# A fused attention and gated MLP block: even and odd positions in paired tiles, products by pairs, and a new order where one chunk hands over to the next

## The chip, the core and the metric

The kernel runs on one core of a Trainium2 chip. The core has a matrix engine (TensorE, in profiles "PE", with its weight loads as "PEld"), a vector engine (VectorE, "DVE"), an activation engine (ScalarE, "ACT"), a third elementwise engine (GpSimd, "POOL") and a queue engine that issues most of the DMA transfers (SyncE, "SP"). Each engine works through its own instructions in order and waits on semaphores for the others. The metric is the device time of one execution in microseconds (us). Lower is better.

## The reference

The input is one sequence of 2048 positions with 512 features, all in float32.

```python
xn = layernorm(x)
# A: 32 heads of 16, each query sees 8 keys: its own position and those 2, 4, ..., 14 earlier
q, k, v = split(xn @ wqkv)
logits = einsum(q, k at pos - 2*w) * 16**-0.5      # masked to -1e9 where pos - 2*w < 0
s = (softmax(logits) applied to v at pos - 2*w) @ wo
# B: an MLP with squared relu, 512 -> 1792 -> 512
h = relu(xn @ w1 + b1)**2
g = silu(h @ w2 + b2)
return x + s * g
```

## The kernel before, in words

Every float32 product is made from three products of a rounded "high" part and a remainder "low" part (`PASSES`): high by high, high by low, low by high. So a 128x512 output with 512 inner features takes 4 x 3 = 12 matmuls. The low part of a tensor is a subtraction on the vector engine or on GpSimd after a rounding copy on the activation engine.

**First phase.** The 2048 positions are 16 tiles of 128 (`NT`). For each tile t the rows of x are loaded (`load_x`, L127), normalised (`mean`, `spread` and `norm` on the activation engine with small steps on GpSimd), transposed on TensorE (`trans`) and split (the high part is the copy in `trans`, the low part `lowx` on the vector engine). Then three products of 12 matmuls give q, k and v (`qkv`, s = 0, 1, 2). Each result goes from PSUM to a staging tile `stg` (an activation copy) and from there to DRAM scratch `sq`, `sk`, `sv` (L395): 256 KB per store, in pieces of 512 bytes, since the scratch is laid out in 4 groups of 128 features. The transposed, split tile itself is stored to `sx` for the later chunks (L537). Four PSUM banks (`psA`) take the products, two (`psT`) the transposes.

**Attention** runs on the vector engine, in 8 units of 256 positions (`UP`). A unit loads its q, and k and v with a halo of 14 positions, with eight consecutive positions in each partition (L197), so a unit needs two finished tiles. It does 4 multiplications and 4 reductions for the logits, the softmax, and 4 multiplications and 4 reductions for the result, which is stored to `so` (L257). `attention()` is a generator: `pump(margin)` takes steps from it as long as a running price of the vector engine's work stays below that of TensorE plus a margin (`SLACK`, `LATE`, `ROOM`). So the order on each engine is fixed when the program is built; only the DMA issues are placed by a scheduler, by when it expects their data.

**Second phase.** The MLP runs in 4 chunks of 512 positions (`C`). For each of the 14 blocks f of 128 hidden features, `up(c, f)` makes 12 matmuls into `ph` (two PSUM banks, `psH`), the activation engine does relu and two squares, and `lowh(f)` on the vector engine makes the low part of `h` out of the same PSUM bank. `up(c, f + 2)` writes that bank again and so waits for `lowh(f)`. `down(pb, f, j)` adds block f to the four outputs `pb` (the four `psA` banks), two blocks behind `up`. `out_product` multiplies attention results by wo into `pw`. At the end of a chunk come `down` of the last two blocks, `gate` (add b2 on the vector engine, silu on the activation engine) and the first two `up` of the next chunk. The chunk's input `xU` (1 MB) is loaded from `sx` right behind the last `up` of the chunk before, into the one buffer `xT` (L401). `finish` multiplies s by g, adds x and stores the rows of the output (L604).

## Time and profile before

| What | us |
|---|---|
| three timed runs | 505.92, 505.95, 511.05 (median 505.95) |
| the profiled execution, its own time | 505.65 |
| its span, first to last instruction | 503.9 |
| TensorE busy | 495.0 (98%) |
| vector engine busy | 414.8 (82%) |
| activation engine busy | 214.2 (43%) |
| GpSimd busy | 113.7 (23%) |
| q, k, v stores | 48 of 256 KB |
| mean granted TensorE clock | 0.998 |

The profiled execution's own time is 1.75 us above its span and 0.3 us below the median of the runs. In timelines a row is a start, a duration and the work, with the idle time of the engine before it and what ended that idle time in brackets; the duration of a group of matmuls includes the modelled end of the last one, so from start to start is the better measure of pace. "SPq" and "ACTq" rows are DMA issues.

### The profile page before, as it was taken

The numbers are of one execution on the slowest core, as the hardware profiler recorded it, in microseconds if no ns is written. First come the engines' busy times: TensorE is split into PE (matmuls) and PEld (weight loads), VectorE is DVE, ScalarE is ACT, GpSimd is POOL, SyncE is SP. The second block draws the span as 40 slices with busy tenths as digits, with TensorE's granted clock in tenths as the row PEclk, the third lists the DMA queues.
The fourth block names the chain that finished last, engine by engine and source line by source line (L and its number), as shares of the span: only waits on it lengthen the run. The fifth ranks groups of instructions, "written<-read, shape, count | busy, mean of one in ns | idle before, by whom it ended". The sixth has DMA issues, their size and how long they took to land.

```text
span 503.9 us, 5987 instructions
## 1 busy us (share of the span) xinstructions
PE 495.0 (98%) x2209; PEld 408.5 (81%) x2209; DVE 414.8 (82%) x327; ACT 214.2 (43%) x393; POOL 113.7 (23%) x127
## 2 busy tenths in 40 slices
PE   7999999999999999999999999999999999999996
PEld 6788888888888888887888888788888888888886
DVE  5309999999999999988899998779999978952245
ACT  3965366663333655512622441263234136123321
POOL 3632165572000589400203000020300002110000
PEclk9999999999999999999999999999999999999999
DMA  8899787899947757461441417044242604021022
GB/s 302 242 285 338 239 280 244 303 312 317 343 140 230 206 160 212 121 261 63 126 157 64 177 42 283 41 148 134 86 174 56 249 1 145 23 85 40 2 85 84
DMA packets 62089, 85.65 MB, mean 170 GB/s; under 512 B 5372, under 2 KB 45676, under 8 KB 59244
## 3 DMA queue, kind: packets, MB, share of 16 engines
q1 hardware_dynamic: 61196, 78.98, 48.4%
q10 hardware_dynamic: 864, 6.29, 3.2%
q8 instruction: 17, 0.28, 0.2%
q14 instruction: 12, 0.10, 0.1%
HBM read 57.94 MB, written 27.32 MB: 169 GB/s over the span
## 4 chain that ended last, share of the span: by engine, by line
PE 91%; DMA 5%; ACT 1%; DVE 1%; issue 0%; ACTq 0%; POOL 0%; POOLq 0%
PE ph L74 30%; PE pb L74 28%; PE pq L74 25%; PE pw L74 7%; DMA xU<-sx 4%; PE pxT L74 2%; DVE xn L74 1%; DMA x<-in_A_x 1%; ACT wq L74 0%; ACT scratch L74 0%; ACT xT L74 0%; ACT stg L74 0%; DVE z L74 0%; ACT xn L74 0%; DVE st L74 0%
## 5 line engine op out<-in xcount | busy, mean ns | idle before, releaser
L74 PE MATMUL pb<-w,h 128*128 128x512 f32 x672 | 161.1, 389 | 0.0
L74 PEld LDWEIGHTS pb<-w,h 128*128 128x128 f32 x672 | 126.2, 188 | 26.2
L74 PE MATMUL ph<-xU,w 128*128 128x512 f32 x504 | 120.8, 389 | 1.5 <-DMA xU<-sx 1.5
L74 ACT ACTIVATE ph<-ph,b1t 128x512 f32<-128x512 f32 x56 | 37.0, 661 | 197.5 <-PE ph L74 184.7
L74 PEld LDWEIGHTS ph<-xU,w 128*128 128x128 f32 x504 | 94.4, 188 | 21.8 <-issue 2.3
L74 PE MATMUL pq<-wq,xt 128*128 128x512 f32 x432 | 101.3, 392 | 0.0
L74 PEld LDWEIGHTS pq<-wq,xt 128*128 128x128 f32 x432 | 80.4, 188 | 16.4
L74 DVE TENSOR_TENSOR pr<-k,q 128x2048 f32<-128x2048 f32 x32 | 75.9, 2370 | 12.2 <-DMA k<-sk 11.8
L74 DVE TENSOR_TENSOR h<-ph,h 128x512 fp32r<-128x512 f32 x56 | 38.4, 685 | 45.7 <-ACT ph L74 45.7
L74 DVE TENSOR_TENSOR pv<-v,L 128x2048 f32<-128x2048 f32 x32 | 73.9, 2310 | 0.6
L74 DVE TENSOR_REDUCE L<-pr 128x128 f32<-128x2048 f32 x32 | 73.1, 2283 | 0.7
L74 DVE TENSOR_REDUCE v<-pv 128x256 f32<-128x2048 f32 x32 | 72.9, 2280 | 0.6
L74 POOL TENSOR_TENSOR z<-z,xr 128x512 f32<-128x512 f32 x12 | 19.2, 1613 | 221.6 <-DVE z L74 214.9
L74 PE MATMUL pw<-wot,oT 128*128 128x512 f32 (+1 forms) x204 | 45.5, 376 | 0.0
L74 ACT ACTIVATE stg<-pq 128x512 f32<-128x512 f32 x48 | 28.3, 595 | 39.0 <-PE pq L74 35.7
L74 PEld LDWEIGHTS pw<-wot,oT 128*128 128x128 f32 x204 | 36.8, 188 | 7.1
L74 POOL TENSOR_TENSOR w<-w1r,w 128x512 fp32r<-128x512 f32 x14 | 28.0, 2003 | 55.4 <-DMA rwo<-in_A_wo 48.9
L74 PE MATMUL ph<-xT,w 128*128 128x512 f32 x168 | 40.5, 390 | 0.0
L74 PEld LDWEIGHTS ph<-xT,w 128*128 128x128 f32 x168 | 31.5, 188 | 6.7
L74 PE MATMUL pq<-wq,xT 128*128 128x512 f32 x144 | 36.4, 410 | 0.0
L74 ACT ACTIVATE h<-ph 128x512 fp32r<-128x512 f32 x56 | 33.5, 599 | 1.8
L74 ACT ACTIVATE ph<-ph 128x512 f32<-128x512 f32 x56 | 33.3, 595 | 0.0
(54 smaller groups left out, 318.7 us busy)
## 6 DMA issues: line engine op xcount, KB each, us to landing
k<-sk SPq DMA_DIRECT2D x8, 1408.0 KB, 8.4
v<-sv SPq DMA_DIRECT2D x8, 1408.0 KB, 7.0
sx<-xt SPq DMA_DIRECT2D x12, 512.0 KB, 4.6
xU<-sx ACTq DMA_DIRECT2D x6, 1024.0 KB, 6.9
x<-in_A_x SPq DMA_DIRECT2D x16, 256.0 KB, 4.1
sq<-stg SPq DMA_DIRECT2D x16, 256.0 KB, 4.4
q<-sq SPq DMA_DIRECT2D x8, 512.0 KB, 4.1
sk<-stg SPq DMA_DIRECT2D x16, 256.0 KB, 4.7
```

Source lines behind the costliest of these rows:

```text
L74: return tc.keep_in_program_order(f(*a, **k))
```

## The change

**Positions.** Tile 2i and tile 2i + 1 no longer hold 128 consecutive positions each. Together they hold 256 consecutive positions, the first tile the even ones and the second the odd ones, so partition p of the pair holds positions 2p and 2p + 1. The loads of x, the residual loads and the output stores use rows two apart. The staging tile now holds one of q, k, v for both tiles of a pair ([P, 4, 2, P], four buffers instead of two of [P, 3, 4, P]), and one DMA of 512 KB stores it, in pieces of 1 KB: 24 stores instead of 48. The loads of the attention result `oq` read 1 KB pieces as well, and the last residual load pieces of 4 KB.

**Order in the first phase.** The products go by pairs: q of both tiles, k of both, v of both, with the transposes, statistics and the splitting of the MLP weights placed anew between them.

**Hand-over of chunks.** `down` of both last blocks now stands ahead of the first two `up` of the next chunk, and `lowh(0)` stands behind the four gates instead of ahead of the second `up`.

```diff
+    def tile_rows(a, t):
+        return a[t // 2 * UP:(t // 2 + 1) * UP, :].rearrange("(p e) d -> e p d", e=2)[t % 2]
...
-    def qkv(t, s, stg, between=None):
+    stgs = {}
+
+    def qkv(t, s, between=None):
+        if t % 2 == 0:
+            stgs[s] = pstg.tile([P, 4, 2, P], F32, name=f"stg{t}_{s}", tag="stg", bufs=4)
         ps = psA(f"pq{t}_{s}")
...
-        A.activation(stg[:, s].rearrange("p g c -> p (g c)"), ps, AF.Copy, scale=0.25 if s == 0 else 1.0)
-        dst = (sq, sk, sv)[s]
-        r0 = t * P + (0 if s == 0 else HALO)
-        dma(dst[:, r0:r0 + P, :].rearrange("g p c -> p g c"), stg[:, s])
-        done_tiles["qk" if s < 2 else "v"] = t + (s > 0)
+        A.activation(stgs[s][:, :, t % 2], ps.rearrange("p (g c) -> p g c", g=4), AF.Copy,
+                     scale=0.25 if s == 0 else 1.0)
+        if t % 2:
+            r0 = (t - 1) * P + (0 if s == 0 else HALO)
+            dst = (sq, sk, sv)[s][:, r0:r0 + UP, :].rearrange("g (p e) c -> p g (e c)", e=2)
+            dma(dst, stgs[s].rearrange("p g e c -> p g (e c)"))
+            done_tiles["qk" if s < 2 else "v"] = t + (s > 0)
...
-    qkv_tile(0, 1, second)
+    qkv(0, 1, lambda: highs(2, 0))
+    trans(2)
+    norm(3)
     lowx(2)
...
-    for t in range(2, NT):
...
+    for a in range(2, NT, 2):
+        b, more = a + 1, a + 2 < NT
...
+        qkv(a, 0)
+        if more:
+            trans(a + 2)
         pump(LATE)
...
+        qkv(b, 0)
+        weights(a - 5)
+        if more:
+            lowx(a + 2)
+            trans(b + 2)
...
+        qkv(a, 1)
...
+        if more:
+            lowx(b + 2)
+        pump(LATE)
+        if not more:
             up(0, 0)
+        qkv(b, 1)
...
+        qkv(a, 2)
...
+        qkv(b, 2)
...
+        if a >= TPC:
+            for t in (a, b):
+                dma(sx[t // TPC][:, t % TPC], xt.pop(t).bitcast(F32))
...
                 for j in range(TPC):
                     down(pb, NF - 2 + i, j)
                 pump()
-                if i:
-                    lowh(0)
+            for i in range(2):
                 up(c + 1, i)
             for j in range(TPC):
                 gate(c, j, pb)
+            lowh(0)
             lowh(1)
             pump()
```

Two places show how instructions move. First TensorE at the hand-over from chunk 0 to chunk 1 (`pw` are the products with wo, `pb0` the outputs of chunk 0, `ph1_0` to `ph1_2` the first `up` products of chunk 1 and `xU1` its input; `h0_13` is the last hidden block of chunk 0). Before:

```order
L74 MATMUL pw1_2050<-wot_1509,oT1_1913 128x512 x12
L74 MATMUL pb0_0_1510<-w12_1744,h0_12_1976 128x512 x3
L74 MATMUL pb0_1_1511<-w12_1744,h0_12_1976 128x512 x3
L74 MATMUL pb0_2_1512<-w12_1744,h0_12_1976 128x512 x3
L74 MATMUL pb0_3_1513<-w12_1744,h0_12_1976 128x512 x3
L74 MATMUL ph1_0_2086<-xU1_2014,w0_637 128x512 x12
L74 MATMUL pb0_0_1510<-w13_1793,h0_13_2017 128x512 x3
L74 MATMUL pb0_1_1511<-w13_1793,h0_13_2017 128x512 x3
L74 MATMUL pb0_2_1512<-w13_1793,h0_13_2017 128x512 x3
L74 MATMUL pb0_3_1513<-w13_1793,h0_13_2017 128x512 x3
L74 MATMUL ph1_1_2121<-xU1_2014,w1_719 128x512 x12
L74 MATMUL ph1_2_2155<-xU1_2014,w2_803 128x512 x12
```

The same place on TensorE after the change:

```order
L74 MATMUL pw1_2034<-wot_1493,oT1_1897 128x512 x12
L74 MATMUL pb0_0_1494<-w12_1728,h0_12_1960 128x512 x3
L74 MATMUL pb0_1_1495<-w12_1728,h0_12_1960 128x512 x3
L74 MATMUL pb0_2_1496<-w12_1728,h0_12_1960 128x512 x3
L74 MATMUL pb0_3_1497<-w12_1728,h0_12_1960 128x512 x3
L74 MATMUL pb0_0_1494<-w13_1777,h0_13_2001 128x512 x3
L74 MATMUL pb0_1_1495<-w13_1777,h0_13_2001 128x512 x3
L74 MATMUL pb0_2_1496<-w13_1777,h0_13_2001 128x512 x3
L74 MATMUL pb0_3_1497<-w13_1777,h0_13_2001 128x512 x3
L74 MATMUL ph1_0_2084<-xU1_1998,w0_661 128x512 x12
L74 MATMUL ph1_1_2101<-xU1_1998,w1_756 128x512 x12
L74 MATMUL ph1_2_2136<-xU1_1998,w2_825 128x512 x12
```

The first product that reads `xU1` has moved behind one more group of 12 matmuls, and the three `ph1` products now follow each other without other work between them.

The vector engine at the same hand-over (`pv` and `v` are attention steps, `z` rows that read `pb` the gates, `h1_0` and `h1_1` the low parts of the next chunk's first two blocks). Before:

```order
L74 TENSOR_TENSOR pv3_1_2115<-v3_1835,L3_1412 128x4x2x256
L74 TENSOR_REDUCE v3_1835<-pv3_1_2115 128x256
L74 TENSOR_TENSOR pv3_2_2118<-v3_1835,L3_1412 128x4x2x256
L74 TENSOR_TENSOR h1_0_2099<-ph1_0_2086,h1_0_2099 128x512
L74 TENSOR_TENSOR z0_0_2138<-pb0_0_1510,b2t_141 128x512
L74 TENSOR_TENSOR z0_1_2141<-pb0_1_1511,b2t_141 128x512
L74 TENSOR_TENSOR z0_2_2144<-pb0_2_1512,b2t_141 128x512
L74 TENSOR_TENSOR z0_3_2147<-pb0_3_1513,b2t_141 128x512
L74 TENSOR_TENSOR h1_1_2134<-ph1_1_2121,h1_1_2134 128x512
L74 TENSOR_TENSOR z0_0_2138<-z0_0_2138,pw0_2037 128x512
```

After:

```order
L74 TENSOR_TENSOR pv3_1_2082<-v3_1819,L3_1396 128x4x2x256
L74 TENSOR_TENSOR z0_0_2118<-pb0_0_1494,b2t_141 128x512
L74 TENSOR_TENSOR z0_1_2121<-pb0_1_1495,b2t_141 128x512
L74 TENSOR_TENSOR z0_2_2124<-pb0_2_1496,b2t_141 128x512
L74 TENSOR_TENSOR z0_3_2127<-pb0_3_1497,b2t_141 128x512
L74 TENSOR_TENSOR h1_0_2097<-ph1_0_2084,h1_0_2097 128x512
L74 TENSOR_TENSOR h1_1_2114<-ph1_1_2101,h1_1_2114 128x512
L74 TENSOR_TENSOR z0_0_2118<-z0_0_2118,pw0_2021 128x512
```

The low part of `h1_0` stands behind the four gates now, and two attention steps have left the stretch ahead of them.

TensorE at the start of the program (`pq0_1` is k of tile 0, `pq1_1` k of tile 1, `pxT2` and `pxT3` the transposes of tiles 2 and 3, `wq1` and `wq2` the split weights of k and v). Before:

```order
L74 MATMUL pq1_0_233<-wq0_111,xT0_170 128x512 x12
L74 MATMUL pq0_1_267<-wq1_112,xT0_170 128x512 x6
L74 MATMUL pxT2_276<-ident_75,xn2_256 128x128 x4
L74 MATMUL pq0_1_267<-wq1_112,xT0_170 128x512 x6
L74 MATMUL pq1_1_301<-wq1_112,xT0_170 128x512 x12
L74 MATMUL pxT3_341<-ident_75,xn3_282 128x128 x4
L74 MATMUL pq0_2_351<-wq2_113,xT0_170 128x512 x12
```

After:

```order
L74 MATMUL pq1_0_231<-wq0_111,xT0_170 128x512 x12
L74 MATMUL pq0_1_266<-wq1_112,xT0_170 128x512 x12
L74 MATMUL pxT2_282<-ident_75,xn2_254 128x128 x4
L74 MATMUL pq1_1_299<-wq1_112,xT0_170 128x512 x12
L74 MATMUL pxT3_339<-ident_75,xn3_288 128x128 x4
L74 MATMUL pq0_2_350<-wq2_113,xT0_170 128x512 x12
```

The transposes of tile 2 have moved from the middle of k of tile 0 to its end.

More of the change, by code (lines that the diff above doesn't have):

```diff
@@ L424, in lowh @@
         V.tensor_sub(h[:, 1], ph, h[:, 0].bitcast(F32))
-    def qkv_tile(t, s, between=None):
-        if s == 0:
-            stgs[t] = pstg.tile([P, 3, 4, P], F32, name=f"stg{t}", tag="stg", bufs=2)
-        qkv(t, s, stgs[t], between)
-    stgs = {}
     sts = [px.tile([P, 6], F32, name=f"st{t}", tag="st", bufs=2) for t in range(2)]
@@ L472, in first @@
         mean(2)
-    def second():
-        highs(2, 0)
-        trans(2)
-        norm(3)
-    qkv_tile(0, 0, first)
+    qkv(0, 0, first)
     lowx(1)
@@ L482, in body @@
     spread(2)
-    qkv_tile(1, 0, lambda: highs(1, 2))
+    qkv(1, 0, lambda: highs(1, 2))
     lows(1, 2)
@@ L491, in body @@
     mean(4)
-    qkv_tile(1, 1, lambda: highs(2, 2))
+    qkv(1, 1, lambda: highs(2, 2))
     lows(2, 2)
@@ L497, in body @@
     next(stream)
-    qkv_tile(0, 2, lambda: norm(4))
+    qkv(0, 2, lambda: norm(4))
     mean(5)
@@ L502, in body, with weights @@
     pump(LATE)
-    qkv_tile(1, 2)
-    mean(6)
+    qkv(1, 2)
+    norm(5)
     pump(LATE)
-    for t in range(2, NT):
-        f = t - 5
-        if 0 <= f < NKEEP:
-            load_w(keep, f)
-        if t + 3 < NT:
-            norm(t + 3)
-        qkv_tile(t, 0)
-        if t + 2 < NT:
-            trans(t + 2)
-        if t + 4 < NT:
-            spread(t + 4)
-        pump(LATE)
-        if t == NT - 1:
+    for a in range(2, NT, 2):
+        b, more = a + 1, a + 2 < NT
+        later = a + 4 < NT
+        def weights(f):
+            if 0 <= f < NKEEP:
+                load_w(keep, f)
+            if 0 <= f - 1 < NKEEP:
+                split_w(f - 1)
+        if later:
+            mean(a + 4)
+        qkv(a, 0)
+        if more:
+            trans(a + 2)
+        pump(LATE)
+        qkv(b, 0)
[3 more added lines that the diff above has]
+            trans(b + 2)
+        if later:
+            mean(b + 4)
+        pump(LATE)
+        qkv(a, 1)
+        if later:
+            spread(a + 4)
+        if more:
+            lowx(b + 2)
+        pump(LATE)
+        if not more:
             up(0, 0)
-        qkv_tile(t, 1)
-        if t + 5 < NT:
-            mean(t + 5)
-        if t == NT - 1:
+        qkv(b, 1)
+        if later:
+            spread(b + 4)
+        if not more:
             pump()
@@ L526, in body @@
             lowh(0)
-        if 0 <= f - 1 < NKEEP:
-            split_w(f - 1)
-        if t + 2 < NT:
-            lowx(t + 2)
+        weights(b - 5)
         pump(LATE)
-        qkv_tile(t, 2)
-        if t == NT - 4:
+        qkv(a, 2)
+        if later:
+            norm(a + 4)
+        pump(LATE)
+        qkv(b, 2)
+        if later:
+            norm(b + 4)
+        if a == NT - 4:
             dma(b1t, b1.rearrange("(f p) -> p f", p=P))
             dma(b2t, b2[None, :].to_broadcast([P, D]))
-        if t >= TPC:
-            dma(sx[t // TPC][:, t % TPC], xt.pop(t).bitcast(F32))
-        pump(LATE if t < NT - 1 else -SLACK)
+        if a >= TPC:
+            for t in (a, b):
+                dma(sx[t // TPC][:, t % TPC], xt.pop(t).bitcast(F32))
+        pump(LATE if more else -SLACK)
     lowh(1)
@@ L595, in load_r @@
         xrs[t] = p2.tile([P, D], F32, name=f"xr{t}", tag="xr", bufs=2)
-        dma(xrs[t], x[t * P:(t + 1) * P, :])
+        dma(xrs[t], tile_rows(x, t))
     def finish(t, eng, xt=None, cols=slice(0, D)):
```

15 lines of the change are left out of this document (8 added, 7 removed).

## The prediction

> **What bounds the kernel now.** I read the page first, then who TensorE waited for, then the timeline of TensorE where the waits fall. The page's span and busy line:
>
> ```profile
> span 503.9 us, 5987 instructions
> PE 495.0 (98%) x2209; PEld 408.5 (81%) x2209; DVE 414.8 (82%) x327; ACT 214.2 (43%) x393; POOL 113.7 (23%) x127
> ```
>
> TensorE is busy for 495.0 of 503.9 us, and the change removes no matmul. So only its 8.9 us without work can be won, unless its pace changes. All of its waits in the profile:
>
> ```profile
> PE ph L74 <- DMA xU<-sx: 1.5, 2, 1.0
> PE pxT L74 <- DVE xn L74: 1.5, 2, 1.2
> PE warm L74 <- POOL mhalf L74: 1.3, 1, 1.3
> PE pxT L74 <- ACT xn L74: 0.8, 1, 0.8
> ```
>
> The list is short and names two things that the change touches: the wait of `ph` for the next chunk's input `xU`, and the wait of the transposes `pxT` for an activation-engine `xn`. No wait is for `sq`, `sk` or `sv`, so halving the number of their stores takes nothing off TensorE directly. The waits for `mhalf` and for the vector engine's `xn` belong to the warm-up and the first two tiles, which the change leaves as they are, as it does the tail behind the last matmul.
>
> **The hand-over of chunks.** TensorE's timeline at the three hand-overs (start, duration, work, idle before and its releaser):
>
> ```profile
> 225.71 2.88 PE L74 MATMUL pb<-w,h 128*128 128x512 f32 x12
> 229.60 3.01 PE L74 MATMUL ph<-xU,w 128*128 128x512 f32 x12 [1.01 <-DMA xU<-sx]
> 232.45 2.88 PE L74 MATMUL pb<-w,h 128*128 128x512 f32 x12
> ...
> 314.05 2.88 PE L74 MATMUL pb<-w,h 128*128 128x512 f32 x12
> 317.40 2.98 PE L74 MATMUL ph<-xU,w 128*128 128x512 f32 x12 [0.48 <-DMA xU<-sx]
> 320.23 2.88 PE L74 MATMUL pb<-w,h 128*128 128x512 f32 x12
> ...
> 404.55 2.88 PE L74 MATMUL ph<-xU,w 128*128 128x512 f32 x12
> 407.27 2.88 PE L74 MATMUL pb<-w,h 128*128 128x512 f32 x12
> ```
>
> The third hand-over has no wait: a group of 12 takes 407.27 - 404.55 = 2.72 us from start to start. By that pace the group behind `ph` was due at 225.71 + 5.44 = 231.15 in the first and came at 232.45, 1.30 late; in the second it was due at 319.49 and came 0.74 late. Together 2.04 us: the 1.5 us of waiting and the slower start of the matmuls behind it. The landings, from the chain of waits:
>
> ```profile
> 218.14 11.33 DMA xU<-sx
> ...
> 306.45 10.82 DMA xU<-sx
> ```
>
> and the low part of the last hidden block on the vector engine, which the moved group of `pb` reads:
>
> ```profile
> 220.79 0.69 DVE L74 TENSOR_TENSOR h<-ph,h 128x512 fp32r<-128x512 f32 x1 [1.25 <-ACT ph L74]
> ```
>
> The landings are at 229.47 and 317.27. In the new order `xU` is first read one group later, at 231.15 and 319.49, so 1.68 and 2.22 us after the landing. I take the whole 2.04 us off. The cover is the moved group of `pb`, which can start at 228.43 (225.71 + 2.72), since its input was there at 221.48. The bounds are nothing, if the transfer comes 1.7 to 2.2 us later, and 2.04.
>
> In exchange `lowh(0)` comes under pressure. The third `up` of the next chunk writes the bank that `lowh(0)` reads. It was due three groups behind the first `up`; now it is due two groups behind, 5.44 us, with the activation engine's three passes and `lowh(0)` in between. The vector engine at the third hand-over, where nothing was disturbed:
>
> ```profile
> 406.67 2.29 DVE L74 TENSOR_TENSOR pv<-v,L 128x2048 f32<-128x2048 f32 x1
> 409.28 0.69 DVE L74 TENSOR_TENSOR h<-ph,h 128x512 fp32r<-128x512 f32 x1 [0.32 <-ACT ph L74]
> 409.89 2.48 DVE L74 TENSOR_TENSOR z<-pb,b2t 128x512 f32<-128x512 f32 x4
> ```
>
> From the first `up` at 404.55 to the end of `lowh(0)` at 409.97 are 5.42 us: all the 5.44 that there are. A release takes a moment more, seen in the chain between the first `xn` on the vector engine and the transposes that wait for it:
>
> ```profile
> 6.62 0.04 issue
> ```
>
> So the third `up` starts about 0.02 us late, and starts cold behind a short wait: the 12 matmuls at 229.60 took 2.85 us from start to start, 0.13 more than 2.72. That is 0.15 us each, 0.45 for three. The bounds are nothing (the two just meet) and one attention step each, which is a rival below. Ahead of `lowh(0)` now stand the four gates, 2.48 us from their start. They need the last `pb`, which ends as the first `up` begins, so they are through 2.5 us behind that at the latest if the vector engine is free, and `lowh(0)` is ready only after 4.73 us (409.28 - 404.55). Queued behind it are `lowh(1)`, the multiplications of `finish` and attention. The vector engine idles some 2 us more in each hand-over, and attention ends that much later. That is covered:
>
> ```profile
> 444.29 2.28 DVE L74 TENSOR_REDUCE v<-pv 128x256 f32<-128x2048 f32 x1
> ...
> 483.33 1.31 DVE L74 STREAM_TRANSPOSE pT<-oq 128x512 f32<-128x512 f32 x2
> ```
>
> The last attention step ends at 446.57 and its result is read at 483.33, so about 36 us stand against some 7, and against a store and a load. The silus come behind both `up` on the activation engine as before.
>
> **The start.** TensorE, GpSimd and the activation engine up to the third tile (the rows of each engine apart):
>
> ```profile
> 11.59 5.85 PE L74 MATMUL pq<-wq,xT 128*128 128x512 f32 x24
> 18.19 0.66 PE L74 MATMUL pxT<-ident,xn 128*128 128x128 f32 x4 [0.75 <-ACT xn L74]
> 18.61 4.46 PE L74 MATMUL pq<-wq,xT 128*128 128x512 f32 x18
> 22.90 0.60 PE L74 MATMUL pxT<-ident,xn 128*128 128x128 f32 x4
> ...
> 17.19 1.27 POOL L74 TENSOR_TENSOR wq<-wqraw,wq 128x512 fp32r<-128x512 f32 x1
> 23.96 1.30 POOL L74 TENSOR_TENSOR wq<-wqraw,wq 128x512 fp32r<-128x512 f32 x1 [0.81 <-ACT wq L74]
> ...
> 20.93 0.80 ACT L74 ACTIVATE xn<-x,shift,rs 128x512 f32<-128x512 f32 x1
> 21.64 0.58 ACT L74 ACTIVATE stg<-pq 128x512 f32<-128x512 f32 x1
> ```
>
> The transposes of tile 2 waited 0.75 us in the middle of k of tile 0; now 6 more matmuls stand ahead of them. At (22.90 - 18.61) / 18 = 0.238 us each, the 29th of the 30 matmuls from 11.59 comes at 18.25. It needs GpSimd's low part of the last quarter of k's weights, there at 18.46, so it waits 0.25. Then two matmuls, 0.42 of transposes and 12 matmuls end at 22.26. Tile 3's `xn`, which ended at 21.73, now stands behind the staging copy of 0.58 and ends by 22.31, about in time. The transposes of tile 3 so start at 22.35, 0.55 us ahead of 22.90. But v's last low part still ends at 25.26, since the activation engine has the same work ahead of it, and the 11th matmul of v would come at about 25.1: 0.2 is given back, and a little for starts behind short waits. I take 0.2 us off, with 0.75 (the whole wait) as the one bound and 0.5 added (one more activation pass on the path) as the other.
>
> **Pairs and pieces.** The first phase has the same products, transposes and copies. The transposes of a pair come one and two products into the pair before it, and their low parts still have four products until they are read, as before. The staging copies have four buffers of one kind each, so a copy reuses a buffer that was stored five products or more ago. SP issues 24 stores fewer; the stores to `sx` stay where their low parts are ready. GpSimd's weight splits move by a product, and it is busy 23%. All of this is hidden behind TensorE's own work, and I cost it at nothing. Its cover is the lead of the vector engine's `lowh` over TensorE, smallest where the first phase ends:
>
> ```profile
> 158.98 0.68 DVE L74 TENSOR_TENSOR h<-ph,h 128x512 fp32r<-128x512 f32 x1
> ...
> 160.43 2.88 PE L74 MATMUL ph<-xT,w 128*128 128x512 f32 x12
> ```
>
> The low part ends at 159.66 and the `up` that writes its bank starts at 160.43, only 0.77 us later. Up to there the vector engine is full from its first attention step on, so this margin is set by when that step starts (SP's issues, then the vector engine, then what transfers took from issue to landing):
>
> ```profile
> 25.23 0.93 SPq L395 DMA_DIRECT2D sk<-stg  x2
> 26.93 0.39 SPq L168 DMA_DIRECT2D sk<-zero  x1
> 30.59 0.55 SPq L197 DMA_DIRECT2D k<-sk  x1
> ...
> 38.04 2.29 DVE L74 TENSOR_TENSOR pr<-k,q 128x2048 f32<-128x2048 f32 x1 [11.77 <-DMA k<-sk]
> ...
> sk<-stg SPq DMA_DIRECT2D x2, 256.0 KB, 4.5
> ```
>
> Two 256 KB stores issued within 0.93 us landed by about 30.2, side by side; the load then waited for the small `zero` transfer. One store of 512 KB at the same moment has the same bytes to move in half as many pieces, so I expect it by 30.2 too, and the first step at 38.0.
>
> **The sum** against the profiled execution: 505.65 - 2.04 + 0.45 - 0.2 = 503.86 us. The median of the runs is 0.3 above the profiled execution, so I forecast 504.2.
>
> **The rivals.**
>
> *The first unit comes late, slower than before.* If the 512 KB store needs twice the 4.5 us, it lands at 34.2 and the k load leaves 3.6 us later than 30.59. The vector engine carries that to the second phase, and 3.6 less the margin of 0.77 - 0.2 is 3.0 us on TensorE: 504.2 + 3.0 = 507.2. It decides from a store that lands later than about 31.2. The two overlapping stores speak against it. [...] Chance 0.08.
>
> *The gates come late.* If the vector engine reaches the gates over 2.25 us behind the start of the first `up` (4.73 less 2.48), `lowh(0)` ends late by the rest. One attention step of 2.29 us more in each hand-over gives 504.2 + 6.9 = 511.1, slower by 1%. Against it: at 408.96 (406.67 + 2.29) that engine was free one microsecond ahead of the last `pb`'s end, and it is still told to stop half a microsecond ahead of it. Chance 0.05.
>
> *The wait only changes its name.* `lowh(0)` costs 0.6 us instead of 0.15 at each hand-over, and the start loses 0.5 instead of gaining 0.2: 504.2 + 1.35 + 0.7 = 506.2, as before. Chance 0.07.
>
> *TensorE gains pace.* Its first products ran slower than later ones:
>
> ```profile
> 23.26 8.68 PE L74 MATMUL pq<-wq,xT 128*128 128x512 f32 x36
> ...
> 58.42 8.43 PE L74 MATMUL pq<-wq,xt 128*128 128x512 f32 x36
> ```
>
> That is 0.25 us per 36, for three such groups; I can't name the cause. If the small pieces of the stores cause it, 0.75 us go: 503.4. Against it: the later group ran beside the same small stores. Chance 0.10.
>
> **The numbers.** The forecast has 0.70, around 504.2: from 503.2 (2.04 and 0.75 off the median, nothing paid) to 505.2. The range of 8 in 10 adds the faster rival's part at the lower end and most of the first two slower ones at the upper: 503.0 to 507.0. A measurement of this kernel can tell about 1% from no change, 500.9 to 511.0. Nearly all cases lie inside: 0.94. Beyond it lie the upper half of the late gates and what I have not seen, 0.05, and 0.01 for faster, since 5 us are more than all the waits that the change touches.
>
> **What would show it.** Right: no `ph` waiting for `xU`, or under 0.3 us; `pw`, `pb`, `pb`, `ph` from start to start at 2.72 per group; a gap of 0 to 0.2 us ahead of the third `ph` of each chunk, released by the vector engine; the first `pr` at 37 to 39 us; TensorE busy for about 495 us. Wrong: TensorE waiting for `h` or for `ph` banks near 150 to 165 us (the first unit came late), a gap of a microsecond or more ahead of the third `ph` (the gates came late), or 36 matmuls of the first phase that take other than 8.3 to 8.5 us.

## The result, and the profile after

The changed kernel took 506.08 us (median of 20 runs, 503.82 to 507.61), and the kernel before, run beside it, 509.26 us (median of 20, 505.78 to 515.11). The ratio is 0.9934, with a 95% interval of 0.9906 to 0.9963: 0.7% faster, inside the 1% that I had set as the bound of what can be told. The same kernel differs by several microseconds from execution to execution, and that turned out to be the subject of this study, so the lowest time stands beside the median in all that follows. From lowest to lowest the change is worth 505.78 - 503.82 = 1.96 us (my sum: 1.79); from median to median 3.2 us. The 505.95 us on which the forecast was built was the median of three runs, two of which were among the quick ones.

The profiled execution of the changed kernel took 507.61 us and is the slowest of the 20. That of the kernel before, 505.65 us, was a quick one. So the two pages compare unequal executions, and a shorter span doesn't show in them. Span and busy line of the changed kernel:

```profile
span 505.8 us, 5934 instructions
PE 495.2 (98%) x2209; PEld 406.4 (80%) x2209; DVE 418.4 (83%) x327; ACT 214.2 (42%) x393; POOL 119.5 (24%) x127
```

All that TensorE waited for in it (total, times, longest):

```profile
PE pxT L74 <- DVE xn L74: 2.0, 2, 1.3
PE pxT L74 <- ACT xn L74: 1.6, 2, 1.4
PE warm L74 <- POOL mhalf L74: 1.3, 1, 1.3
PE pq L74 <- ACT stg L74: 0.9, 1, 0.9
PE pq L74 <- DVE wq L74: 0.4, 1, 0.4
PE pq L74 <- POOL wq L74: 0.2, 1, 0.2
```

The wait of `ph` for `xU` is gone, and so is that of tile 2's transposes. New are 1.6 us for an activation-engine `xn` in the middle of the first phase and 0.9 us for a staging copy `stg`. The two waits for `wq` lie at the start; the one for GpSimd (0.17 us at 18.33) is the one that I had forecast there at 0.25. TensorE's timeline at the first and the third hand-over:

```profile
223.50 5.60 PE L74 MATMUL pw<-wot,oT 128*128 128x512 f32 x24
228.94 5.60 PE L74 MATMUL pb<-w,h 128*128 128x512 f32 x24
234.38 8.50 PE L74 MATMUL ph<-xU,w 128*128 128x512 f32 x36
242.71 2.88 PE L74 MATMUL pb<-w,h 128*128 128x512 f32 x12
...
408.80 8.58 PE L74 MATMUL ph<-xU,w 128*128 128x512 f32 x36
417.22 2.88 PE L74 MATMUL pb<-w,h 128*128 128x512 f32 x12
```

From start to start, `pw` and `pb` run at full pace (5.44 us per 24). The 36 matmuls of three `up` take 8.33 us at the first and 8.42 at the third, against 8.16: that is the pressure of `lowh(0)` on the third `up`, 0.17 + 0.17 + 0.26 = 0.60 us in the three hand-overs. I had 0.45.

The first phase holds what I had not forecast. The vector engine's first attention step, an exponential of the activation engine, the vector engine's `lowh(1)`, and TensorE's waits (the rows of each engine apart):

```profile
39.71 2.29 DVE L74 TENSOR_TENSOR pr<-k,q 128x2048 f32<-128x2048 f32 x1 [13.62 <-DMA x<-in_A_x]
...
162.79 0.68 DVE L74 TENSOR_TENSOR h<-ph,h 128x512 fp32r<-128x512 f32 x1
...
131.81 0.63 ACT L74 ACTIVATE L<-L 128x512 f32<-128x512 f32 x1 [10.47 <-DVE L L74]
...
67.84 0.66 PE L74 MATMUL pxT<-ident,xn 128*128 128x128 f32 x4 [1.45 <-ACT xn L74]
...
132.98 11.18 PE L74 MATMUL pq<-wq,xt 128*128 128x512 f32 x48 [0.95 <-ACT stg L74]
...
163.53 3.01 PE L74 MATMUL ph<-xT,w 128*128 128x512 f32 x12
```

The first step started at 39.71 us; in the profile before it was 38.04. The exponential of a unit has a fixed place among the activation engine's instructions. Here it stood at the head of that engine's row for 10.47 us until the vector engine had the logits. Behind it stood the staging copies that empty TensorE's four banks, and at 132.98 TensorE had waited 0.95 us for one. At 163.47 (162.79 + 0.68) `lowh(1)` ends, and `up(0, 3)`, which needs its bank, starts at 163.53; in the profile before that was 160.43. So TensorE reached the second phase 3.1 us later. Only the last 0.24 us of that are for `lowh(1)`: the group ahead started at 160.57, so `up(0, 3)` was due at 163.29. The rest are the waits for `xn` (1.45 and 0.18) and `stg` (0.95) and the slower starts behind them (0.3 us, by subtraction). At the end of the third hand-over TensorE was still 1.8 us later (417.22 against 415.43), so it made up 1.3 us there: the 2.04 less the 0.60 paid at `lowh(0)`, nearly.

**Two theories** follow. Theory H: the hand-over edit gives the 1.4 to 2 us between the lowest times, as forecast; what a kernel with the old hand-over loses is the wait for `xU` and, in some executions, a halved clock with it (0.50 at the wait of 2.64 us below). Theory L: what lies between one execution and another is the lateness of the vector engine, which the activation engine's fixed order passes on to TensorE. The rivals are that pairs and pieces give the gain, and that the spread has some cause outside this chain.

### The profile page after: what moved, and what is told of

The parts are those of the page before. It is cut to its first block, busy times and chain, and to the rows that moved or that the text cites. A ratio compares the mean times of both kernels' runs of the same rounds, so it can differ in the third digit from the quotient of the medians.

```text
span 505.8 us, 5934 instructions
## 1 busy us (share of the span) xinstructions
PE 495.2 (98%) x2209; PEld 406.4 (80%) x2209; DVE 418.4 (83%) x327; ACT 214.2 (42%) x393; POOL 119.5 (24%) x127
## 4 chain that ended last, share of the span: by engine, by line
PE 70%; DVE 17%; issue 4%; ACT 3%; DMA 3%; POOL 3%; POOLq 0%; ACTq 0%; DVEq 0%
PE pb L74 30%; PE ph L74 29%; PE pw L74 9%; DVE L L74 5%; DVE pr L74 5%; DMA x<-in_A_x 3%; PE pq L74 3%; DVE v L74 2%; DVE pv L74 2%; ACT scratch L74 1%; POOL rs L74 1%; POOL wq L74 1%; DVE xt L74 1%; ACT stg L74 1%; DVE xn L74 1%
## 5 line engine op out<-in xcount | busy, mean ns | idle before, releaser
L74 DVE TENSOR_TENSOR pr<-k,q 128x2048 f32<-128x2048 f32 x32 | 77.0, 2407 | 14.0 <-DMA x<-in_A_x 13.6
L74 DVE TENSOR_TENSOR pv<-v,L 128x2048 f32<-128x2048 f32 x32 | 75.6, 2362 | 0.5
L74 POOL TENSOR_TENSOR z<-z,xr 128x512 f32<-128x512 f32 x12 | 21.2, 1778 | 219.3 <-DVE z L74 212.5
L74 POOL TENSOR_TENSOR w<-w1r,w 128x512 fp32r<-128x512 f32 x14 | 22.1, 1580 | 60.9 <-DMA rwo<-in_A_wo 49.6
L74 POOL TENSOR_TENSOR w<-w2r,w 128x512 fp32r<-128x512 f32 x14 | 34.5, 2466 | 0.0
```

Of the source, the lines that this page charges most:

```text
L74: return tc.keep_in_program_order(f(*a, **k))
```

## The experiments

The runs came in three groups, each on another chip and beside its own runs of the kernel before: lowest and median there 505.15 and 508.70 (33 runs) in the first group, 505.06 and 505.77 (27) in the second, 505.36 and 508.00 (31) in the third. Medians of different groups are therefore compared with care, and lowest times are the safer measure. All runs in one table, in us:

| Group | Kernel | runs | lowest | median | highest |
|---|---|---|---|---|---|
| 1 | hand-over edit alone | 12 | 503.80 | 505.14 | 510.03 |
| 1 | changed, old hand-over | 12 | 506.04 | 506.70 | 509.09 |
| 1 | changed, stores of 256 KB in 512 B pieces | 12 | 503.80 | 506.01 | 507.05 |
| 1 | changed, two multiplications less | 10 | 503.95 | 504.21 | 504.83 |
| 2 | before, two multiplications less | 12 | 505.10 | 505.73 | 508.92 |
| 2 | before with the hand-over edit, two less | 10 | 503.70 | 504.00 | 504.33 |
| 2 | changed, two multiplications more | 4 | 509.69 | 510.35 | 511.05 |
| 2 | changed, later planned start | 10 | 503.05 | 503.91 | 504.15 |
| 3 | before with the hand-over edit, later planned start | 8 | 503.81 | 503.88 | 504.12 |
| 3 | before, later planned start | 12 | 504.48 | 504.88 | 505.42 |
| 3 | changed, again | 12 | 503.57 | 505.22 | 506.31 |
| 3 | changed, later planned start, split `pb` | 12 | 503.96 | 504.27 | 505.60 |

### The hand-over edit alone

```diff
 (kernel before)
                 pump()
-                if i:
-                    lowh(0)
+            for i in range(2):
                 up(c + 1, i)
             for j in range(TPC):
                 gate(c, j, pb)
+            lowh(0)
             lowh(1)
```

> The kernel before with the hand-over edit alone: the last group of pb moved ahead of the next chunk's ups, lowh(0) behind the gates; tiles, stores and start as before. Theory A (the hand-over edit brings the whole gain of the quickest executions): the quickest execution is 1.4 to 2.0 us below the quickest of the kernel before (2.04 taken off, 0.6 paid at lowh(0) by the profile after), ph no longer waits for xU, and the later executions lie as far behind as those of the kernel before do. Theory B (the gain comes from pairs and pieces, the hand-over only trades one wait for another): no difference within 0.5 us, and a wait ahead of the third ph of each chunk that adds up to about 2 us.

Its lowest time is 503.80 us, 1.35 below that of the kernel before, and as low as the whole change gets. So theory A of the expectation holds at the low end: the hand-over edit alone brings it. But its highest is 510.03. The profiled execution (507.90 us) shows one such late case, on TensorE and in a table of stretches (start and end; length and busy us and instructions of each engine; granted clock; share of the DMA engines; GB/s):

```profile
132.40 15.41 PE L74 MATMUL pq<-wq,xt 128*128 128x512 f32 x60 [2.22 <-ACT stg L74]
...
132.40:133.40 1.00, 1.00 (x2) 0.83 (x3) 1.00 (x1) 1.00 (x3) 0.00 (x0) 0.50 0.93 394
133.40:134.40 1.00, 1.00 (x4) 0.78 (x3) 0.96 (x2) 0.90 (x2) 0.00 (x0) 0.50 0.88 332
134.40:135.40 1.00, 1.00 (x4) 0.81 (x3) 1.00 (x1) 0.00 (x0) 0.00 (x0) 0.50 1.10 325
```

A wait of 2.22 us for a staging copy, and 3.4 us at half the clock (0.50), from just before its end (132.2 to 135.6): the 60 matmuls took 15.41 us, where the same 60 take 13.87 without a wait (in the profile of the later planned start, below). The wait so cost 1.5 us on top of itself.

### The changed kernel with the old hand-over

```diff
 (changed kernel)
                 pump()
-            for i in range(2):
+                if i:
+                    lowh(0)
                 up(c + 1, i)
             for j in range(TPC):
                 gate(c, j, pb)
-            lowh(0)
             lowh(1)
```

> The changed kernel with the old hand-over: pairs of tiles, 1 KB pieces and the new start remain. Theory A: its quickest execution is within 0.4 us of the quickest of the kernel before, and ph waits for xU again, 1.0 and 0.5 us. Theory B: it keeps most of the 2 us. Whatever the difference of the medians beyond that of the quickest executions is (3.2 against 2.0 us for the whole change), it shows here and not in the hand-over alone, if the pairs or pieces make late executions rarer or shorter.

Its lowest time, 506.04, is 0.9 above that of the kernel before, outside the 0.4 that theory A allowed, and its median 2.0 below. The profiled execution (509.09 us) had an early vector engine (first step at 37.34 us) and no wait between 25 and 170 us; its loss is at the hand-over, in TensorE's timeline and the table of stretches:

```profile
231.03 4.58 PE L74 MATMUL ph<-xU,w 128*128 128x512 f32 x12 [2.64 <-DMA xU<-sx]
...
232.00:233.00 1.00, 1.00 (x4) 0.79 (x3) 1.00 (x1) 0.00 (x0) 0.00 (x0) 0.50 0.00 0
233.00:234.00 1.00, 1.00 (x4) 0.80 (x3) 0.78 (x1) 0.00 (x0) 0.00 (x0) 0.50 0.00 0
```

The wait for `xU` is back, 2.64 us, again with the clock halved (0.50): 12 matmuls in 4.58 us against 2.88, 1.7 lost on top of the wait. By the pace of 2.72 us per group the `pb` behind `ph` was due at 230.95 and came at 235.44; at the second hand-over, with a wait of 0.56, it came 0.84 late. Without these 5.3 us the execution would lie at 503.8 (an estimate). So pairs and pieces alone don't bring the low times: the old hand-over takes them away. Why it cost every execution of this kernel over 2 us, where the kernel before at its best loses some 1.4, one profile doesn't say.

### The changed kernel with small stores

```diff
 (changed kernel, in qkv, after the staging copy)
+        r0 = t // 2 * UP + (0 if s == 0 else HALO)
+        dst = (sq, sk, sv)[s][:, r0:r0 + UP, :].rearrange("g (p e) c -> e p g c", e=2)[t % 2]
+        dma(dst, stgs[s][:, :, t % 2])
         if t % 2:
-            r0 = (t - 1) * P + (0 if s == 0 else HALO)
-            dst = (sq, sk, sv)[s][:, r0:r0 + UP, :].rearrange("g (p e) c -> p g (e c)", e=2)
-            dma(dst, stgs[s].rearrange("p g e c -> p g (e c)"))
             done_tiles["qk" if s < 2 else "v"] = t + (s > 0)
```

> The changed kernel, but q, k and v of each tile stored by itself, 256 KB in 512 B pieces (even and odd rows kept, order of products kept). My prediction costed the pieces at nothing: then it equals the changed kernel within 0.3 us, the store of unit 0's k lands in about 4.5 us and the vector engine's first step starts within 0.5 us of where it did. Rival (the pieces matter, by the transfers' load): the first step starts 1 us or more later, and TensorE's waits near 67, 133 and 157 us grow by as much.

503.80 and 506.01 us against the changed kernel's 503.82 and 506.08 in its own runs: the size of the stores and pieces is worth nothing here. The 12 times lie in two clusters, five at 503.8 to 504.5 and seven at 506.0 to 507.1, as those of the changed kernel do. The compute engines have the same instructions in the same order as in the changed kernel, and the profiled execution (504.38 us) is of the low cluster, so its profile serves below as that of an early execution. Its first attention step came at 37.48 us, 2.23 ahead of the profile of the changed kernel and not within the 0.5 that I expected; but in a second profile of the changed kernel (below) it came at 37.92, so that difference is not the doing of the stores.

### Two multiplications less in the first unit

```diff
 (changed kernel; the same in the kernel before and in that with the hand-over edit)
-            V.tensor_mul(pr, kv, qv)
+            if u == 0 and s < 2:
+                clock["V"] += price("V", "tensor_mul", (pr,), {})
+            else:
+                V.tensor_mul(pr, kv, qv)
...
-                in_=pr.rearrange("p w (g d) -> p w g d", d=HD), axis=AX.X, op=OP.add)
+                in_=(kv if u == 0 and s < 2 else pr).rearrange("p w (g d) -> p w g d", d=HD), axis=AX.X, op=OP.add)
```

This leaves out two of the four products of k and q in the first unit: the reductions there sum k itself, and the output is another. The planner still counts their price, so the order of everything else stays. In the changed kernel:

> The changed kernel with the first two multiplications k*q of unit 0 left out (the logits there are sums of k alone, so the first part of the attention's result is another), everything else in its order: the vector engine runs 4.6 us ahead of where it was. Theory L (an exponential of the activation engine that waits for late logits keeps the staging copies behind it, and TensorE waits for their banks): all executions lie at about the quickest of the changed kernel, 503.3 to 504.2 us, the activation engine's wait for L falls from 31 to about 5 us, and TensorE waits for neither xn nor stg nor lowh(1) between 60 and 165 us. Rival (the spread has another cause, such as the pace of the chip or transfers at the end): the executions lie in the same two clusters as those of the changed kernel, near 504 and 506.

All ten executions lie between 503.95 and 504.83 us. The activation engine's wait for logits, in the list of waits, falls from 30.9 us (the changed kernel) to

```profile
ACT L L74 <- DVE L L74: 10.5, 5, 5.3
```

and TensorE waits nowhere between 25 and 170 us. The second cluster is gone when the vector engine comes 4.6 us earlier: theory L. In the kernel before:

> The kernel before with the first two multiplications k*q of unit 0 left out (the logits there are sums of k alone, so the first part of the attention's result is another): the vector engine 4.6 us ahead. What is left of its spread comes from the hand-over. Theory H (xU lands 11 to 13 us after its issue, TensorE waits for it 1 to 2.6 us, and behind a wait of 2 us or more its clock stands at 0.5 for 3 us, which costs another 1.6): 505.2 us at the best, executions up to 508 or 509, and in the profile either a wait for xU of about 1 us and full clock behind it, or of over 2 us and half the clock. Rival (the spread was that of the late vector engine alone): all executions at 505.2 to 506.

505.10 to 506.48 us for eleven of the twelve and 508.92 for one; theory H with the spread that it asked for, though mostly at its lower end. The median is that of the kernel before in the same group (505.73 against 505.77), whose runs were mostly quick there; what is missing in these 12 runs is its upper part, up to 513.29. TensorE's timeline shows the wait:

```profile
230.41 2.97 PE L74 MATMUL ph<-xU,w 128*128 128x512 f32 x12 [2.15 <-DMA xU<-sx]
```

With this one of 2.15 us the clock stayed at 1.00 (2.97 us for 12), where with one of 2.22 us it stood at 0.50. In the kernel before with the hand-over edit:

> The kernel before with the hand-over edit alone and the same two multiplications of unit 0 left out: no wait for xU and no late vector engine. Theory H and theory L together (the only two sources of the spread are the wait for xU and the late vector engine): all executions within 1 us of each other, at 503.8 to 504.8 us; against the same kernel without the hand-over edit 1.4 us at the best execution (2.04 taken off, 0.6 paid) and 2 to 4 us at the median. The forecast of the start (-0.2) and of pairs and pieces (0) asks for 0.2 us more than the changed kernel with the same multiplications left out, whose median is 504.21.

503.70 to 504.33 us. With both sources removed, ten executions lie within 0.63 us. Against the same kernel with the old hand-over this is the cleanest price of the edit: 505.10 - 503.70 = 1.40 us at the lowest and 505.73 - 504.00 = 1.73 at the median. My sum for the hand-over was 2.04 - 0.45 = 1.59. The 0.2 us that the expectation asked for the start doesn't show in the times (504.00 here, 504.21 in the changed kernel).

### Two multiplications more

```diff
 (changed kernel)
+            for _ in range(2 if (u, s) == (0, 0) else 0):
+                tc.keep_in_program_order(nc.vector.tensor_mul(pr, kv, qv))
             V.tensor_mul(pr, kv, qv)
```

> The changed kernel with two multiplications of unit 0 done twice more, 2.29 us each, so that the vector engine is 4.6 us later from there on and nothing else is changed. Theory L: TensorE's waits for xn and stg near 67 and 133 us and for lowh(1) near 163 us grow by together about 4 us, some of them pass 2 us and halve the clock behind them, and the time is 508 to 512 us, more than the 4.6 that the vector engine is later. Rival (the vector engine has slack in the first phase and the gap at the bank of xn has another cause): within 1 us of the changed kernel, 504 to 507.

509.69 to 511.05 us (four executions), 4.3 us above the changed kernel's median of 506.08. In TensorE's timeline the wait at a transpose and the second one at a staging copy are the same two as in the changed kernel, and a staging copy at 65 us is new:

```profile
65.02 3.01 PE L74 MATMUL pq<-wq,xt 128*128 128x512 f32 x12 [1.11 <-ACT stg L74]
...
69.79 0.66 PE L74 MATMUL pxT<-ident,xn 128*128 128x128 f32 x4 [1.76 <-ACT xn L74]
...
134.97 11.19 PE L74 MATMUL pq<-wq,xt 128*128 128x512 f32 x48 [0.94 <-ACT stg L74]
...
165.50 2.79 PE L74 MATMUL ph<-xT,w 128*128 128x512 f32 x11
```

Its first step began at 37.03 and the doubled work took 4.62, so the work proper began at 41.65, against 39.71 in the changed kernel's profile: 1.94 us later, and `up(0, 3)` came at 165.50 against 163.53: 1.97. In these two profiles, once the vector engine is late, TensorE pays one for one. No wait here passed 2 us (the longest is 1.76) and the clock stayed at 1.00; that part of the expectation did not come.

### A later planned start

```diff
 (changed kernel; the same in the kernel before and in that with the hand-over edit)
-        not_before(clock["PE"] + 8000)
+        not_before(clock["PE"] + 15000)
```

This number says from when the planner counts the vector engine as busy with the first unit. Rows of the activation engine in program order, the changed kernel first, then with the edit: the exponential of the first unit moves behind three staging copies and an `xn`.

```
53 L74 ACTIVATE L<-L 128x512
54 L74 ACTIVATE stg<-pq 128x4x128
...
56 L74 ACTIVATE stg<-pq 128x4x128
...
58 L74 ACTIVATE stg<-pq 128x4x128
59 L74 ACTIVATE xn<-x,shift,rs 128x512

53 L74 ACTIVATE stg<-pq 128x4x128
...
55 L74 ACTIVATE stg<-pq 128x4x128
...
57 L74 ACTIVATE stg<-pq 128x4x128
58 L74 ACTIVATE xn<-x,shift,rs 128x512
59 L74 ACTIVATE L<-L 128x512
```

> The changed kernel with one number of the order changed: the planner counts the vector engine's first attention step from 15 us instead of 8 us after the point where it is released, which is nearer to where it starts in the trace, so every exponential stands 2 to 6 rows later in the activation engine's order, behind staging copies and xn that were kept waiting. Theory L: the copies no longer wait for the vector engine, TensorE has no wait for stg or xn between 60 and 135 us, and the executions lie together at 503.6 to 504.5 us, 1.5 us or more under the changed kernel's median. Rival (the vector engine's lateness reaches TensorE through lowh(1) at 163 us whatever the activation engine's order): the two clusters stay, 504 and 506 us.

503.05 to 504.15 us, median 503.91, and the ratio to the kernel before 0.9945 (0.9923 to 0.9967) beside runs of it that were mostly quick ones. It leaves nothing out, has the lowest time of all, and is ahead of both kernels. Activation engine and TensorE:

```profile
132.01 0.64 ACT L74 ACTIVATE L<-L 128x512 f32<-128x512 f32 x1 [4.26 <-DVE L L74]
...
121.40 13.87 PE L74 MATMUL pq<-wq,xt 128*128 128x512 f32 x60
```

The exponential still waits, 4.26 us, and starts no earlier than the 131.81 of the changed kernel. But the copies that TensorE needs are ahead of it, and TensorE runs its 60 matmuls without a gap. So the wait in itself is harmless; what stands behind it is not. The rival, that lateness reaches TensorE whatever the activation engine's order, falls. The same number in the kernel before with the hand-over edit:

> The kernel before with the hand-over edit and the later start of the planner's vector engine (15 us for 8); tiles, pieces and start of the kernel before. If the wait for xU and the late vector engine are the only sources of the spread, and pairs and pieces are worth no more than the 0.2 us of the start: executions between 503.7 and 504.6 us, median at most 0.5 us above the 503.91 of the changed kernel with the later start. If the pairs or pieces are needed for steadiness: executions beyond 505.5 us remain, with waits for xn or stg near 67 and 133 us.

503.81 to 504.12 us, median 503.88 against 503.91 for the changed kernel: at the median pairs, pieces and the new start add nothing to it that these runs can see. The lowest time of the changed kernel was 0.76 us lower (503.05), on another chip. And in the kernel before alone:

> The kernel before with the later start of the planner's vector engine alone; the old hand-over remains. Theories L and H: the first phase has no wait for stg, and for xn in the middle none; what is left is the wait for xU, so 505.1 to 506.6 us, with single executions near 508 to 509 where that wait passes 2 us and the clock is halved behind it, about as the kernel before with two multiplications left out (median 505.73). Rival (the hand-over's wait shrinks when the vector engine is on time): 504 us.

504.48 to 505.42 us, lower than expected. In its profile the first two hand-overs have no wait, and the third has one whose releaser the profile does not name; TensorE's timeline, and the transfers near it (size of one, median from issue to landing):

```profile
403.56 3.00 PE L74 MATMUL ph<-xU,w 128*128 128x512 f32 x12 [1.19 <-issue]
...
xU<-sx ACTq DMA_DIRECT2D x2, 1024.0 KB, 10.5
```

The two halves of `xU` were issued there between 391.53 and 392.79 us, so landings near 403 fit. With the later start the hand-over edit is worth 504.88 - 503.88 = 1.0 us, so its price depends on how soon `xU` comes: the rival of this run holds in part. Why `xU` came sooner at the other two I did not find out.

### The changed kernel again

> The changed kernel as it is, beside the others on the same chip, for a profile of one more execution and a median that compares directly. Theory L: executions near 504 us and near 506 us. If the profile falls on one near 506, it shows waits for xn, stg or lowh(1) between 60 and 165 us that add up to about 2 us at full clock, and none of over 0.3 us after 170; if on one near 504, none of either, and a first attention step before 38.5 us.

503.57 to 506.31 us, six near 504 and six near 506, median 505.22, ratio 0.9934 (0.9906 to 0.9962), as in the first comparison. The profile (505.80 us) is of the later six. It has two small waits in the middle of the first phase, 0.18 and 0.95 us, at the same places as in the first profile, and some 0.2 more for `lowh(1)`: 1.4 in all, where I expected about 2. TensorE at `up(0, 3)`, in the early execution with small stores and then here:

```profile
160.26 2.88 PE L74 MATMUL ph<-xT,w 128*128 128x512 f32 x12
...
161.79 3.01 PE L74 MATMUL ph<-xT,w 128*128 128x512 f32 x12
```

But its first attention step was not late: 37.92 us, only 0.44 behind the 37.48 of the early execution. So my expectation that a step before 38.5 us goes with an early execution is wrong: 0.44 us at the start had become 1.53 us on TensorE. Where it grew can be read from the vector engine's timelines. First the early execution (small stores), with the activation engine's exponential at the end:

```profile
71.65 2.90 DVE L74 TENSOR_TENSOR pr<-k,q 128x2048 f32<-128x2048 f32 x1
...
87.20 2.29 DVE L74 TENSOR_TENSOR pr<-k,q 128x2048 f32<-128x2048 f32 x1
89.53 2.29 DVE L74 TENSOR_REDUCE L<-pr 128x128 f32<-128x2048 f32 x1
...
105.01 0.69 DVE L74 TENSOR_TENSOR L<-L,sm 128x512 f32<-128x512 f32 x1
...
126.75 0.63 ACT L74 ACTIVATE L<-L 128x512 f32<-128x512 f32 x1 [7.18 <-DVE L L74]
```

Then the later one, the same instructions, and two of GpSimd:

```profile
72.10 3.36 DVE L74 TENSOR_TENSOR pr<-k,q 128x2048 f32<-128x2048 f32 x1
...
88.35 3.11 DVE L74 TENSOR_TENSOR pr<-k,q 128x2048 f32<-128x2048 f32 x1
91.49 2.29 DVE L74 TENSOR_REDUCE L<-pr 128x128 f32<-128x2048 f32 x1
...
106.98 1.78 DVE L74 TENSOR_TENSOR L<-L,sm 128x512 f32<-128x512 f32 x1
...
88.01 1.30 POOL L74 TENSOR_TENSOR w<-w1r,w 128x512 fp32r<-128x512 f32 x1 [4.88 <-ACT w L74]
89.27 3.35 POOL L74 TENSOR_TENSOR w<-w2r,w 128x512 fp32r<-128x512 f32 x1
...
130.09 0.63 ACT L74 ACTIVATE L<-L 128x512 f32<-128x512 f32 x1 [10.47 <-DVE L L74]
```

The vector engine never waits in this stretch. Its multiplications take 2.29 us when alone (at 83.70) and up to 3.36 when GpSimd's splits of the MLP weights run; a split takes 1.30 beside a reduction (at 70.76) and 3.35 beside a multiplication (at 89.27). The reductions, which read one tensor, stay at 2.29, also beside a split (at 91.49). By 126.75 the later execution is 3.34 us behind instead of 0.44. Summed over the stretched rows of the two timelines (six in the later, four in the early execution) 4.12 us against 1.24 are lost, and the difference of 2.88 is nearly all of the 2.90 by which the lag grew. So a small shift decides which multiplications meet a split. The split that started at 89.27 ended at 92.62, 1.16 us behind the end of the multiplication at 91.46; by what means the two engines hold each other up, no run shows. That this is what separates the two clusters in every execution is read from one profile of each, and no run tested it by moving the splits.

### The first `up` inside the last group of `pb`

```diff
 (changed kernel with the later planned start)
                 for j in range(TPC):
+                    if i and j == 2:
+                        up(c + 1, 0)
                     down(pb, NF - 2 + i, j)
                 pump()
-            for i in range(2):
-                up(c + 1, i)
+            up(c + 1, 1)
```

> The changed kernel with the later start of the planner's vector engine, and the first up of the next chunk placed in the middle of the last group of pb, 6 matmuls earlier, so that the third up stands 6.8 us behind the first and not 5.44. My reading of the 0.6 us paid at lowh(0): the 36 matmuls of up, from third to third, no longer take 8.33 but 8.16 us, 0.2 each, 0.6 in all. But xU is first read 1.36 us earlier, 0.6 to 1.2 us ahead of its landing where that takes 11 to 13 us, which gives back 0 to 1.3 us at the first hand-over. Net between 503.3 and 504.6 us; a wait for xU under 1.3 us in the profile, and none ahead of the third ph. Rival (the 0.6 us has another cause than the distance from the first up): the time of three ups stays at 8.33 and more.

503.96 to 505.60 us, median 504.27: 0.4 more than with the groups whole. TensorE's timeline and the vector engine's at the first hand-over, then TensorE's at the second and the third:

```profile
236.48 2.96 PE L74 MATMUL ph<-xU,w 128*128 128x512 f32 x12 [0.32 <-DVE h L74]
...
233.26 2.47 DVE L74 TENSOR_TENSOR z<-pb,b2t 128x512 f32<-128x512 f32 x4
235.66 0.68 DVE L74 TENSOR_TENSOR h<-ph,h 128x512 fp32r<-128x512 f32 x1
...
320.89 5.84 PE L74 MATMUL ph<-xU,w 128*128 128x512 f32 x24
326.57 2.88 PE L74 MATMUL pb<-w,h 128*128 128x512 f32 x12
...
408.17 5.60 PE L74 MATMUL ph<-xU,w 128*128 128x512 f32 x24
413.61 1.75 PE L74 MATMUL pb<-w,h 128*128 128x512 f32 x7
```

At the third the loss is gone, as I read it: 24 matmuls in 5.44 us from start to start. At the second they take 5.68, so 0.24 is lost, no less than with the groups whole. At the first the third `ph` still waits 0.32 us: `lowh(0)` now stands behind the gates, which start only when the last `pb` is done, and it ends at 236.34 where it was due by 236.00. So the distance from the first `up` was half the story; the other half is the place of `lowh(0)` behind the gates. The `pb` behind it came at 239.29, 0.57 later than due (233.28 + 5.44). So 0.57 + 0.24 = 0.81 us are lost in the three hand-overs, where the profile of the later planned start has 0.17 + 0.18 + 0.21 = 0.56. These 0.25 us are most of the 0.30 between the two profiled executions (504.13 and 503.83). No wait for `xU` shows in this profile. What made its slowest executions, 505.0 to 505.6, is open.

## Why the prediction was right, and where it was not

**The range and the size held**: 506.08 lies in 503.0 to 507.0 and within 1% of the time before. The point forecast of 504.2 is met by the quick executions (503.8 to 504.2) and missed by the median, by 1.9 us. That the median lies in the range is in part luck: the base of 505.95 was 3.3 us under the median of 20 runs, the gain was 1.4 larger than forecast, and the lateness that puts the median 1.9 above the point was costed at nothing. Only the room left for other rivals holds it.

**Hand-over (-2.04 + 0.45): right in mechanism and nearly in size.** No `ph` waits for `xU`; `pw`, `pb`, `pb` follow at 2.72 us. Measured without the first phase's trouble it is worth 1.4 to 1.7 us, forecast 1.59. The term of `lowh(0)` was 0.60 instead of 0.45. What I had not seen is that the wait removed can be far larger than the 1.0 and 0.5 us of the one profile: in kernels with the old hand-over waits of 2.15 and 2.64 us were seen, the second with the halved clock (0.50), and across the profiles transfers of up to 12.9 us.

**Start (-0.2): right in the traces, too small for the times.** With the new start (small stores) the transposes of tile 3 began at 22.39 us against 22.90 before: 0.51 earlier, forecast 0.55. By 31.57 against 31.77 most of it was given back, as forecast. `up(0, 3)` came at 160.26 against 160.43: 0.17 us. Two more pairs of undisturbed profiles, both with the new hand-over and each with the first phase of the changed kernel and of that before, have 0.16 (two multiplications less) and 0.30 (later planned start). No comparison of times shows it.

**Pairs and pieces (0): right in time with the new hand-over, wrong in the reason.** With the later planned start, with and without them, the medians are 503.91 and 503.88. (With the old hand-over the lowest time with them was 0.9 us higher, from the wait for `xU`.) But the step that failed is its cover: "this margin is set by when that step starts", and "I expect it by 30.2 too, and the first step at 38.0". The store did land as expected (4.9 us for 512 KB, against 4.5 for 256 KB). But the load of `k` left 0.27 us later and took 8.7 us instead of 7.3, the step came at 39.71 instead of 38.04, and the margin of 0.77 us was gone. In the second profile of the changed kernel the step did come at 37.92, as forecast, and `up(0, 3)` was still 1.36 us behind the 160.43 of the profile before: so the start of that step does not set the margin by itself, since multiplications that GpSimd stretched used up the rest. I had taken the margin of one quick execution for that of the kernel. And I had looked for its end only at `lowh`, at 159 us, where the activation engine's wait for the logits, 6.18 us ahead of the exponential at 60 us in the profile before, already stood in front of the staging copies.

**The rival "the first unit comes late"** has the right place and the wrong trigger. It asked for a store that lands after 31.2 us. The store did not double: the rival's 3.0 us rest on twice the 4.5 us, which was my estimate; no run shows it for this store, and in the profile it took 4.9 us. But late first units occur with either first phase, from a load of `k` that leaves late (at 31.80 us in the profile of the hand-over edit alone, whose stores are of 256 KB) or lands late, and from collisions with GpSimd, and they reach TensorE about as the rival said: 41.65 against 39.71 us at the first step, 1.97 us at `up(0, 3)`. With 0.08 I gave that road far too little.

**The other rivals.** The gates do come late in one place, at the first hand-over of the last experiment, and make `lowh(0)` 0.34 us late there, not the 2.3 of an attention step. TensorE did not gain pace: 132.98 and 11.18 us for 48 matmuls show none. "The wait only changes its name" came true in part, and where I did not look: an execution that no longer waits for `xU` may wait for `xn` and `stg` instead. That its 506.2 is near the median is chance, since neither of its terms was seen: `lowh(0)` cost 0.60 us in all, not 0.6 each time, and the start lost nothing.

**The extra gain at the median**, 3.2 us where the lowest times differ by 2.0, fits the removal of those larger waits, as far as the runs go: with the hand-over edit alone the median is 3.6 below that of the kernel before in the same group, with pairs and the old hand-over 2.0, with both 2.8 to 3.2. These do not add up, since each median is a mixture of early and late executions; how much pairs take from the late ones (highest time 510.03 with the hand-over edit alone, 507.61 with the whole change) I leave open.

## What to carry to other kernels

An in-order engine that serves two others must not have an instruction that waits for the one ahead of those that the other needs: with the exponential behind the copies, its wait of 4.26 us cost nothing here. Where a planner fixes the order, its idea of when an engine starts has to agree with the trace; one number, 15 us for 8, was worth 1.3 to 2.2 us at the median of the changed kernel and took away its spread. And a margin is read from several executions: one profile of a kernel whose times differ by some us shows one of its cases.

## What the runs showed of the hardware

**TensorE's granted clock fell to 0.50 at three of the waits.** With waits of 2.22 and 2.64 us it stood at 0.50 for 3.4 us (132.2 to 135.6 and 231.5 to 234.9), and they cost 1.5 and 1.7 us more than themselves; with waits of 2.15, 1.76 and 1.45 us it stayed at 1.00. So the 2 us that my expectations took for a border is not one in these traces, since 2.15 lies above it. A sixth case, in the kernel before with the later planned start, speaks against the length of a wait as what decides. TensorE's timeline there and the table of stretches:

```profile
6.63 0.76 PE L74 MATMUL pxT<-ident,xn 128*128 128x128 f32 x4 [1.79 <-DVE xn L74]
...
8.00:9.00 1.00, 1.00 (x4) 0.65 (x3) 0.92 (x3) 1.00 (x4) 0.67 (x2) 0.50 1.03 393
```

This wait of 1.79 us, shorter than 2.15, ended at 6.63, and from 8 to 9 us the clock stood at 0.50; its mean over the first 12.6 us was 0.8 to 0.9. What decides whether the clock falls, these six cases don't show.

**The vector engine and GpSimd stretch each other**: 2.29 to 3.36 us for a multiplication of 128x2048, 1.30 to 3.35 us for a split of 128x512. It made 0.44 us of difference into 3.3 us within 90 us of program.
